# One query ring buffer, joined value products, two more blocks transposed by DMA, and a new order of work in a fused attention and gMLP kernel

## The chip, the cores and the metric

The kernel runs on one core of a Trainium2 chip. The metric is the device time of one execution in microseconds (us); for the kernel before it is the median of three runs.

## What is computed

`x` is 2048 tokens by 512 channels in bf16. After one layernorm without weights, two branches run on the same normalized input `xn`, and their outputs are added to `x`:

```python
def _A_ref(x, wqkv, wo):                 # 32 heads of 16, window of 256 tokens
    qkv = (x @ wqkv).reshape(B, S, 3, H, Dh) ...
    scores = einsum('bhqd,bhkd->bhqk', q, k) * Dh ** (-0.5)
    mask = (i - j >= 0) & (i - j < 256)
    p = softmax(where(mask, scores, -1e9))
    return einsum('bhqk,bhkd->bhqd', p, v) ... @ wo

def _B_ref(x, w_in, w_sp, b_sp, w_out):  # gMLP, 2 x 688 features
    z = gelu(x @ w_in); z1 = z[..., :688]; z2 = layernorm(z[..., 688:])
    g = einsum('ts,bsf->btf', w_sp, z2) + b_sp[None, :, None]
    return (z1 * g) @ w_out

xn = layernorm(x); return x + _A_ref(xn, ...) + _B_ref(xn, ...)
```

## The kernel before

The 2048 tokens are 16 blocks of 128 (`n`, also `qb` and `kb` for query and key blocks). The 32 heads are 4 groups `G` of 8; a group's projections are made for 512 tokens at a time (`grp`, 0 to 3).

**First stage (lines 211 to 373), in the order of the program.** SyncE (the queue SPq) loads `x` in pieces `xs` (two blocks each) and the two halves of `w_in` in two pieces each (`load_x`, L196; `load_win`, L204), then `wqkv`, the rest of `x`, and the output weights `wo_sb` and `w_out_sb` (L331 to L335). For each block, VectorE makes the statistics (`stats`, L254, L255, L119; the root is taken on GpSimd, L120) and the normalized block (`norm`, L260). Blocks 0 to 7 (`X_DMA = 8`) are transposed on TensorE (`transpose_x`, tile `tp`, L274) and copied out by ScalarE (L277); blocks 8 to 15 are transposed by a DMA that SPq issues (L265). Either way the result is `xnT`. `do_z(n, half)` multiplies a block with half of `w_in` in eight matmuls, four of 512 columns and four of 176 (tile `zs`, L285), and ScalarE applies the gelu (L293). TensorE works through this in program order: `z` of block `n`, half 1, comes two rounds after `norm(n)` has been issued. Twelve matmuls on zeros (`warm_up`, `N_WARM = (9, 3)`, L246) run ahead of and between the first two transposes. The first nine of 48 projections are done in this stage.

**Second stage: one list of tokens, `ORDER` (lines 49 to 65), played in order (lines 573 to 596).** Every engine gets its instructions in that order and keeps it. The tokens:

- `qIIe` is `scores(i, e)`: tile `i` of 45 holds four (key block, query block) pairs of the 180 that lie in the window, in the order of `BLOCKS`: per group, per key block, query blocks `kb`, `kb+1`, `kb+2`. For each of four heads, matmuls with 32 rows each (L483) fill half a tile `S` of the PSUM ring `ps_s`; two tiles are taken per call, and two exponentials on ScalarE (L491) of 128 x 1024 each turn them into `E`. Neighbouring pairs of one key block whose queries lie side by side in one tile `q` go into one matmul (`segs`); a query block with `qb % 4 == 0` starts a new one, as the next 512 queries are another tile.
- `mII` masks the tile: GpSimd for the diagonal blocks (L502), VectorE for `qb == kb + 2` (L507).
- `aGW`, `AGW`, `BGW`, `CGW` are `values`: for query blocks 2W and 2W+1 of group G, value products with 32 output rows each (L531), one per block pair, head and half: 1440 matmuls of 128 columns in all. `a` uses the one-bank pool `ps_y`, `A` and `C` a place of the ring `ps_s`. `divide` follows (L548 to L554), and `t` is `finish` (L565).
- `pKGg` and `PKGg` are the other projections (`proj`), in `ps_y` or in the ring.
- A number is that many `mix` steps (L402, 512 in all): the products with `w_sp`, 128 x 344 each. Sixteen of them end with an evacuation on VectorE (L409); at a row's end its `uT` is transposed by DMA (L425).
- `o` and `O` are halves of an output block (L433, L439), added to `x` on VectorE (L444) and stored (L445; blocks 13 to 15 from ScalarE's queue, the others from SPq).

`ps_s` has three places, `ps_y` and `ps_g` (for `mix`) one each. A score tile therefore waits until the exponential of the tile three places back in the ring has read it. Query tiles come from the pool `qp` of six, one per projection, in the order of the tokens.

Of the kernel before, what the change touches and what calls it, by code (L numbers as in the profile page):

```python
# [8 lines left out]
P = 128  # L9
BF = mybir.dt.bfloat16  # L10
# [5 lines left out]
D = 512  # L16
# [3 lines left out]
FH = 688  # L20
FQ = FH // 2
NB = S_TOK // P
# [6 lines left out]
Z_RANGES = [(0, 512), (512, FH)]  # L29
NRING = 6  # L30
EBUFS = 7
X_DMA = 8
LAST = 128
ONB = 4
N_WARM = (9, 3)

# [18 lines left out]
q171 t pq23 m15 2 t 2 q180 1 pq13 3 q181 6 m16 2 q190 a12 4 q191 1 m18 pq22 m19 3 q200 2 pv22 1  # L55
t 5 q201 a13 3 q210 2 m17 2 pq30 1 t q211 4 t 4 q220 pk23 C14 B15 q221 1 pk22 3 q230 7 m21 2
q231 3 pv23 q240 1 m22 m20 3 pv21 q241 5 Pk30 3 q250 t 4 a16 A17 q251 pv20 3 q260 8 m23 3 q261 2
pq31 q270 1 m25 m24 6 a20 q271 9 Pv31 q280 pv30 4 q281 1 m26 1 pk33 q290 9 Pq33 1 t q291 a21 t
A22 m27 4 q300 8 q301 4 pk32 q310 2 m28 5 t 2 q311 7 a23 q320 7 m29 7 q321 2 pk31 Pq32 1 m30 1
q330 6 t 4 q331 4 a24 q340 2 m33 m32 9 t q341 5 pv32 A25 q350 9 q351 5 m31 2 pv33 q360 t 8 q361  # L60
6 t 1 m34 1 a30 A26 t t q370 2 t t 1 a27 q371 5 m37 5 q380 2 o 1 q381 o m36 m35 10 q390 O O q391
t 6 a31 A32 q400 7 t 5 q401 3 o 1 q410 t o 4 m40 q411 o m39 3 q420 m38 o q421 5 O 4 O a33 q430
# [6 lines left out]
def kernel(  # L69
# [12 lines left out]
    nc = tc.nc  # L82
# [4 lines left out]
    pers = ctx.enter_context(tc.tile_pool(name="pers", bufs=1))  # L87
# [23 lines left out]
    qp = ctx.enter_context(tc.tile_pool(name="qp", bufs=NRING))  # L111
# [10 lines left out]
    q_t, k_t, v_t = {}, {}, {}  # L122

    def bank(name, ring):
        if ring:
# [3 lines left out]
    def proj(kind, G, grp, on_act=False, ring=False):  # L129
        m = bank("m", ring)  # L130
        if kind == "v":
            for j in range(4):
                n = 4 * grp + j
                for c in range(NDC):
                    nc.tensor.matmul(  # L135
                        m[:, j * P : (j + 1) * P], lhsT=xnT[:, c, n * P : (n + 1) * P],
                        rhs=wqkv[:, c, 2 * D + G * P : 2 * D + (G + 1) * P],
                        start=(c == 0), stop=(c == NDC - 1),
                    )
            t = v_bufs[(4 * G + grp) % NRING]  # L140
            v_t[(G, grp)] = t
            dst = t[:].rearrange("p n h a d -> p (n h) a d")[:, :, 0:3:2, :]
            src = m.rearrange("p (h e d) -> p h e d", e=2, d=DH)
            if on_act:
                nc.scalar.copy(out=dst, in_=src)
            else:
                nc.vector.tensor_copy(out=dst, in_=src)
            return
        w0 = (D if kind == "k" else 0) + G * P
        for c in range(NDC):  # L150
            nc.tensor.matmul(  # L151
                m, lhsT=wqkv[:, c, w0 : w0 + P], rhs=xnT[:, c, grp * 512 : (grp + 1) * 512],
                start=(c == 0), stop=(c == NDC - 1),
            )
        if kind == "q":
            t = qp.tile([P, 512], BF, name="q")
            q_t[(G, grp)] = t
            if on_act:
                nc.scalar.copy(out=t[:], in_=m)
            else:  # L160
                nc.vector.tensor_copy(out=t[:], in_=m)
# [15 lines left out]

    with tc.tile_pool(name="win_pool", bufs=1) as winp, tc.tile_pool(
# [152 lines left out]
        nc.sync.dma_start(out=wo_sb[:], in_=A_wo.rearrange("(c p) n -> p c n", p=P))  # L331
        nc.sync.dma_start(
            out=w_out_sb[:, 0:5, :], in_=B_w_out[0:640, :].rearrange("(c p) n -> p c n", p=P)
        )
        nc.sync.dma_start(out=w_out_sb[0 : FH - 5 * P, 5, :], in_=B_w_out[5 * P : FH, :])  # L335
        norm(2)
        do_z(1, 1)
        transpose_x(2)
# [123 lines left out]
    E_tiles = {}  # L462

    def scores(i, e):
# [4 lines left out]
        E = E_tiles[i]  # L469
        segs = []  # L470
        for j, (G, kb, qb) in enumerate(blocks):
            if segs and segs[-1][1:3] == [G, kb] and qb % 4:
                segs[-1][4] += 1
            else:
                segs.append([j, G, kb, qb, 1])
        tiles = []
        for pr in range(2):
            S = ps_s.tile([P, 2, 512], F32, name="S", tag="S")
            tiles.append(S)
            for h2 in range(2):  # L480
                s = 2 * pr + h2
                for j, G, kb, qb, w in segs:
                    nc.tensor.matmul(  # L483
                        S[:, h2, j * P : (j + w) * P],
                        lhsT=k_t[(G, kb // 4)][32 * s : 32 * s + 32, e, (kb % 4) * P : (kb % 4 + 1) * P],
                        rhs=q_t[(G, qb // 4)][32 * s : 32 * s + 32, (qb % 4) * P : (qb % 4 + w) * P],
                        start=True, stop=True,
                    )
        for pr in range(2):
# [26 lines left out]
    def values(G, w, home):  # L516
# [5 lines left out]
            tile2 = ps_s.tile([P, 2, 512], F32, name="o_t2", tag="S")  # L522
            Tb = tile2[:, 0, :]
        T = Tb.rearrange("p (e q) -> p e q", e=2)
        for j, qb in enumerate((2 * w, 2 * w + 1)):
            kbs = [kb for kb in (qb - 2, qb - 1, qb) if kb >= 0]
            for e in range(2):
                for kb in kbs:
                    i, b = INDEX[(G, kb, qb)]
                    for s in range(4):  # L530
                        nc.tensor.matmul(  # L531
                            T[32 * s : 32 * s + 32, e, j * P : (j + 1) * P],
                            lhsT=v_t[(G, kb // 4)][:, kb % 4, s, e : e + 2, :].rearrange("p a d -> p (a d)"),
                            rhs=E_tiles[i][:, 2 * s + e, b, :],
                            start=(kb == kbs[0]),
                            stop=(kb == qb),
                        )
        if home == "C":
            pair.append((G, w, tile2))
            return  # L540
# [26 lines left out]

    load_wsp(0)
    load_wsp(1)
    tokens = ORDER.split()  # L570
    last_proj = max(i for i, t in enumerate(tokens) if t[0] in "pP")
    xres = {}
# [54 lines left out]
```

## Time and profile before

| | |
|---|---|
| median of 3 runs | 267.56 us (267.45 to 267.75) |
| the profiled execution's own time | 268.1 us |
| its span, first to last instruction | 266.1 us |
| busy: TensorE, its weight loads, VectorE, ScalarE, GpSimd | 258.6, 147.1, 197.3, 206.0, 123.6 us |
| granted TensorE clock over the span | 1.00 |
| first exponential | 56.0 us into the span |

In the profile PE is TensorE's matmuls, PEld its weight loads, DVE VectorE, ACT ScalarE, POOL GpSimd, SPq SyncE's queue. A row of the timeline has the start, the length and the engine, line and tiles of some like instructions run together (`x8` is eight); the length reaches to the modelled end of the last one, which lies after the start of the next row, because matmuls are pipelined. The time that a piece of TensorE work takes is therefore read from start to start. A row of the chain of waits has the start, the length and the piece of work.

### The profile page before, as it was taken

The numbers are of one execution on the slowest core, as the hardware profiler recorded it, in microseconds if no ns is written. First come the engines' busy times: TensorE is split into PE (matmuls) and PEld (weight loads), VectorE is DVE, ScalarE is ACT, GpSimd is POOL, SyncE is SP. The second block draws the span as 40 slices with busy tenths as digits, with TensorE's granted clock in tenths as the row PEclk, the third lists the DMA queues.
The fourth block names the chain that finished last, engine by engine and source line by source line (L and its number), as shares of the span: only waits on it lengthen the run. The fifth ranks groups of instructions, "written<-read, shape, count | busy, mean of one in ns | idle before, by whom it ended". The sixth has DMA issues, their size and how long they took to land.

```text
span 266.1 us, 8418 instructions
## 1 busy us (share of the span) xinstructions
PE 258.6 (97%) x3661; PEld 147.1 (55%) x3694; DVE 197.3 (74%) x384; ACT 206.0 (77%) x235; POOL 123.6 (46%) x140
## 2 busy tenths in 40 slices
PE   7999999999999999999999999999999999999995
PEld 2565665645455547554656656655665454554543
DVE  5999999567766778968788888767777658568542
ACT  3677767699999999999999899897899789553000
POOL 4334454115645256746637493156573617247200
PEclk9999999999999999999999999999999999999999
DMA  6992325700504050251312054033059972423733
GB/s 204 350 363 55 61 40 112 88 2 2 110 15 98 2 111 21 63 46 38 81 31 52 17 66 81 2 81 83 15 130 272 143 123 59 98 74 30 150 91 89
DMA packets 60132, 23.63 MB, mean 89 GB/s; under 512 B 51216, under 2 KB 59584, under 8 KB 60096
## 3 DMA queue, kind: packets, MB, share of 16 engines
q1 hardware_dynamic: 59472, 22.70, 38.5%
q8 instruction: 29, 0.48, 0.7%
q10 hardware_dynamic: 576, 0.39, 0.5%
q0 software_dynamic: 48, 0.00, 0.3%
q14 instruction: 7, 0.06, 0.1%
HBM read 8.41 MB, written 2.10 MB: 39 GB/s over the span
## 4 chain that ended last, share of the span: by engine, by line
PE 88%; ACT 7%; DMA 2%; issue 1%; SPq 1%; DVE 0%; ACTq 0%
PE gf L402 28%; PE zs L285 14%; PE S L483 11%; PE m L151 8%; PE o_t L531 8%; PE fo L439 8%; ACT E L491 7%; PE m L135 5%; PE fo L433 5%; DMA w_in_sb<-in_B_w_in_dram 2%; PE tp L274 1%; ACT L491 0%; DVE xnT L444 0%; SPq L194 0%; SPq L196 0%
## 5 line engine op out<-in xcount | busy, mean ns | idle before, releaser
L491 ACT ACTIVATE E<-S 128x1024 bf16<-128x1024 f32 x180 | 168.4, 1056 | 18.1 <-PE S L483 14.1
L402 PE MATMUL gf<-z_all,wspT 128*128 128x344 bf16 x512 | 94.2, 310 | 0.0
L502 POOL TENSOR_SCALAR_AFFINE_SELECT E<-E 128x1024 bf16<-128x1024 bf16 x64 | 79.3, 1264 | 18.1 <-ACT E L491 18.0
L402 PEld LDWEIGHTS <-wspT 128*128 128x128 bf16 x512 | 44.2, 98 | 33.8 <-issue 10.5
L554 POOL TENSOR_TENSOR o_norm<-o_c,rsum 128x256 bf16<-128x256 f32 x32 | 23.2, 726 | 77.3 <-DVE rsum L552 77.3
L507 DVE TENSOR_TENSOR E<-E,fmask 128x1024 bf16<-128x1024 bf16 x56 | 51.9, 954 | 1.6 <-ACT E L491 1.5
L285 PE MATMUL zs<-w_in_sb,xnT 128*128 128x176 bf16 (+1 forms) x250 | 39.7, 307 | 0.7 <-DMA w_in_sb<-in_B_w_in_dram 0.4
L483 PE MATMUL S<-q,k 32*128 32x128 bf16 (+2 forms) x888 | 38.5, 251 | 0.8 <-ACT E L491 0.8
L293 ACT ACTIVATE z_all<-zs 128x688 bf16<-128x688 f32 x32 | 23.8, 744 | 12.5 <-PE zs L285 12.5
L151 PE MATMUL m<-xnT,wqkv 128*128 128x512 bf16 x110 | 31.3, 379 | 0.9
L285 PEld LDWEIGHTS <-xnT 128*128 128x128 bf16 x256 | 22.2, 98 | 15.3 <-issue 0.6
L409 DVE SCALAR_TENSOR_TENSOR z_all<-gf,b_all,z_all 128x344 bf16<-128x344 f32 x32 | 18.2, 570 | 15.8 <-PE gf L402 15.7
L483 PEld LDWEIGHTS <-k 32*128 32x128 bf16 x888 | 15.2, 92 | 25.7 <-issue 23.7
L548 DVE STREAM_TRANSPOSE o_c<-o_t 128x512 f32<-128x512 f32 x32 | 22.3, 698 | 8.2 <-PE o_t L531 8.0
L531 PE MATMUL o_t<-E,v 128*32 128x128 bf16 x1440 | 24.5, 220 | 0.0
L531 PEld LDWEIGHTS <-v 128*32 128x32 bf16 x1440 | 20.3, 97 | 6.2 <-issue 6.0
L439 PE MATMUL fo<-w_out_sb,uT 128*128 128x512 bf16 (+2 forms) x98 | 23.0, 366 | 0.3 <-issue 0.2
L444 DVE TENSOR_TENSOR xnT<-fo,xnT 128x512 bf16<-128x512 f32 (+2 forms) x17 | 11.1, 657 | 13.6 <-PE fo L439 13.6
L171 DVE TENSOR_TENSOR k<-m,emask 128x1024 bf16<-128x1024 f32 x13 | 15.8, 1219 | 6.3 <-PE m L151 6.3
L151 PEld LDWEIGHTS <-wqkv 128*128 128x128 bf16 x128 | 12.0, 98 | 11.3 <-issue 0.9
L120 POOL TENSOR_TENSOR rstdx<-rs_v,negh 128x1 f32<-128x1 f32 x16 | 10.3, 646 | 16.1 <-DVE rs_v L119 14.7
L298 DVE BATCH_NORM_STATS2 st<-z_all 128x6 f32<-128x344 bf16 x32 | 14.9, 506 | 3.7 <-ACT z_all L293 3.7
(51 smaller groups left out, 177.4 us busy)
## 6 DMA issues: line engine op xcount, KB each, us to landing
xnT<-in_A_x_dram SPq DMA_DIRECT2D x4, 512.0 KB, 6.4
xs<-in_A_x_dram SPq DMA_DIRECT2D x7, 256.0 KB, 7.5
out_dram<-xnT SPq DMA_DIRECT2D x13, 128.0 KB, 1.7
wqkv<-in_A_wqkv_dram SPq DMA_DIRECT2D x1, 1536.0 KB, 7.2
w_in_sb<-in_B_w_in_dram SPq DMA_DIRECT2D x4, 344.0 KB, 5.1
w_out_sb<-in_B_w_out_dram SPq DMA_DIRECT2D x1, 640.0 KB, 10.4
wo_sb<-in_A_wo_dram SPq DMA_DIRECT2D x1, 512.0 KB, 9.1
xs<-in_A_x_dram SPq DMA_DIRECT2D x2, 128.0 KB, 2.1
```

Source lines behind the costliest of these rows:

```text
L151: nc.tensor.matmul(m, lhsT=wqkv[:, c, w0 : w0 + P], rhs=xnT[:, c, grp * 512 : (grp + 1) * 512], start=(c == 0), stop=(c == NDC - 1),)
L285: nc.tensor.matmul(zp[:, lo:hi], lhsT=xnT[:, c, n * P : (n + 1) * P], rhs=w_in_sb[:, c, f0 + lo : f0 + hi], start=(c == 0), stop=(c == NDC ...
L293: nc.scalar.activation(out=dst[:, n, 0:FH], in_=zp[:, 0:FH], func=ACT.Gelu_apprx_tanh)
L402: nc.tensor.matmul(gf[:, 0:FQ], lhsT=wsp_tiles[n][:, c, :], rhs=z2_all[:, c, lo : lo + FQ], start=(c == 0), stop=(c == NB - 1),)
L439: nc.tensor.matmul(fo[:, c0:c1], lhsT=uT_tiles[n][:, c, :], rhs=w_out_sb[:, c, c0:c1], start=False, stop=(c == NFC - 1),)
L483: nc.tensor.matmul(S[:, h2, j * P : (j + w) * P], lhsT=k_t[(G, kb // 4)][32 * s : 32 * s + 32, e, (kb % 4) * P : (kb % 4 + 1) * P], rhs=q_ ...
L491: nc.scalar.activation(out=E[:, j : j + 3 : 2, 0:nb, :].rearrange("p h b c -> p h (b c)"), in_=tiles[pr][:, :, 0 : nb * P], func=ACT.Exp, ...
L502: nc.gpsimd.affine_select(out=E[:, :, j, :], in_=E[:, :, j, :], pattern=[[0, 8], [1, P]], compare_op=ALU.is_ge, fill=0.0, base=0, channel_ ...
L507: nc.vector.tensor_tensor(out=E[:, :, j, :], in0=E[:, :, j, :], in1=fmask[:].unsqueeze(1).to_broadcast([P, 8, P]), op=ALU.mult,)
L531: nc.tensor.matmul(T[32 * s : 32 * s + 32, e, j * P : (j + 1) * P], lhsT=v_t[(G, kb // 4)][:, kb % 4, s, e : e + 2, :].rearrange("p a d -> ...
L548: nc.vector.transpose(out=C[:, 0 : 32 * DH], in_=Tb)
L554: nc.gpsimd.tensor_tensor(out=o_n[:], in0=c_o.rearrange("p e q d -> p q e d"), in1=rsum[:].rearrange("p e q -> p q e").unsqueeze(3).to_bro ...
```

## The change

- **Queries.** The pool `qp` goes. All six tiles lie side by side in one buffer `q_ring`; group `G`, part `grp` has place `(4 * G + grp) % 6`. In `scores`, a matmul now goes on over the edge of 512 queries unless the ring wraps.
- **Value products.** `values` goes through half `e`, then key block, then query block, and joins the two query blocks of one key block into one matmul of 256 columns where they lie side by side in one tile `E`. Only the first step of a bank has `start`.
- **First stage.** `X_DMA` is 6: blocks 6 and 7 are transposed by DMA. The second piece of `w_in`'s half 1 is issued ahead of `load_x(1)`. One more warm-up matmul. `wo_sb` and `w_out_sb` are loaded after the first two `load_wsp`, just ahead of the token list.
- **End.** The first part of block 15 is stored from SPq instead of ScalarE's queue.
- **Order.** A new token list of the same work.

```diff
-X_DMA = 8
+X_DMA = 6
-N_WARM = (9, 3)
+N_WARM = (10, 3)
 ORDER = """
-pq10 Pk03 q000 1 pq03 2 q001 4 pk10 q010 9 m00 q011 pv11 m01 4 q020 4 pk11 q021 8 q030 a00 7
-q031 m02 1 pk12 2 q040 5 q041 1 m03 pq12 t 1 m04 3 q050 8 q051 pv03 4 q060 pq11 3 m05 q061 2 a01
-2 q070 9 q071 pv10 m06 4 q080 pk13 2 m07 1 q081 3 A02 2 q090 t a03 q091 4 A04 m08 q100 5 q101 3
-pk20 q110 5 t 3 t q111 pq20 4 q120 1 m10 pv13 4 q121 3 m11 a05 t q130 4 pv12 q131 8 t 1 q140 1
-m09 1 m12 1 pq21 q141 4 A06 a07 q150 8 q151 m13 a10 1 t 4 q160 3 pk21 2 q161 8 q170 m14 a11 6
...
-q330 6 t 4 q331 4 a24 q340 2 m33 m32 9 t q341 5 pv32 A25 q350 9 q351 5 m31 2 pv33 q360 t 8 q361
-6 t 1 m34 1 a30 A26 t t q370 2 t t 1 a27 q371 5 m37 5 q380 2 o 1 q381 o m36 m35 10 q390 O O q391
...
-m42 O 4 t 1 O 4 m41 1 o 2 q431 3 o 1 q440 C34 B35 t o q441 t m44 1 m43 1 o O 2 O 1 O 1 O 1 O 1
-A36 a37 2 O 1 t 1 o 1 o O t O 3 o o O O o o
+pv11 Pk03 q000 1 pq03 2 q001 2 pq10 1 q010 9 m00 q011 1 pk10 q020 3 m01 2 a00 1 q021 10 q030
+pk11 4 m02 q031 10 q040 2 pv03 q041 4 m03 t 1 pk12 q050 6 m04 1 q051 1 a01 3 q060 pk13 3 m05
+q061 4 a02 1 q070 8 q071 a03 1 t 3 q080 pv10 2 m07 2 q081 pq11 3 m06 1 q090 pq12 4 q091 a04 3
+m08 q100 2 pk20 2 q101 9 q110 pv12 1 t 1 m10 3 q111 1 pv13 1 m09 q120 5 pq21 q121 3 t 1 a05 m11
+q130 2 m12 8 q131 pq20 4 q140 t t 2 pk21 q141 3 A06 a07 A10 q150 4 m13 7 q151 2 pq13 q160 m14 6
...
+Pq33 3 a24 q321 2 t 7 t q330 3 pq32 t Pk31 q331 pv33 4 q340 2 m32 3 m33 3 q341 4 pv32 m34 1 q350
+2 t 10 q351 3 a30 A25 t A26 a27 q360 10 q361 3 t o 1 q370 1 m35 1 o m36 q371 3 m37 5 t q380 3 o
...
+q441 3 O m44 O o o t 5 A37 1 t O O t 2 o o 1 O O 6 O 1 O O O O O
 """
+    q_ring = pers.tile([P, NRING * 512], BF, name="q_ring")
         if kind == "q":
-            t = qp.tile([P, 512], BF, name="q")
+            at = (4 * G + grp) % NRING * 512
+            t = q_ring[:, at : at + 512]
         load_x(0, split=True)
         load_win(1, 0, 2)
+        load_win(1, 2, 4)
         load_x(1)
-        load_win(1, 2, 4)
-        nc.sync.dma_start(out=wo_sb[:], ...)          # these three go ...
-        nc.sync.dma_start(out=w_out_sb[:, 0:5, :], ...)
-        nc.sync.dma_start(out=w_out_sb[0 : FH - 5 * P, 5, :], ...)
-        (nc.scalar if n >= NB - 3 else nc.sync).dma_start(
+        (nc.scalar if n >= NB - 3 and c1 == D else nc.sync).dma_start(
         for j, (G, kb, qb) in enumerate(blocks):
-            if segs and segs[-1][1:3] == [G, kb] and qb % 4:
+            at = (4 * G + qb // 4) % NRING * 4 + qb % 4
+            if segs and segs[-1][1:3] == [G, kb] and at:
                 segs[-1][4] += 1
-                        rhs=q_t[(G, qb // 4)][32 * s : 32 * s + 32, (qb % 4) * P : (qb % 4 + w) * P],
+                        rhs=q_ring[32 * s : 32 * s + 32, at * P : (at + w) * P],
-        for j, qb in enumerate((2 * w, 2 * w + 1)):   # then e, kb, s: one matmul of 128 columns each
+        steps = []
+        for e in range(2):
+            for kb in range(max(0, 2 * w - 2), 2 * w + 2):
+                for qb in range(max(kb, 2 * w), min(kb + 3, 2 * w + 2)):
+                    i, b = INDEX[(G, kb, qb)]
+                    if qb > max(kb, 2 * w) and steps[-1][2:4] == [i, b - 1]:
+                        steps[-1][5] += 1
+                    else:
+                        steps.append([e, kb, i, b, qb - 2 * w, 1])
+        for n, (e, kb, i, b, j, l) in enumerate(steps):
+            for s in range(4):
+                nc.tensor.matmul(
+                    T[32 * s : 32 * s + 32, e, j * P : (j + l) * P],
+                    lhsT=v_t[(G, kb // 4)][:, kb % 4, s, e : e + 2, :].rearrange("p a d -> p (a d)"),
+                    rhs=E_tiles[i][:, 2 * s + e, b : b + l, :].rearrange("p b c -> p (b c)"),
+                    start=(n == 0), stop=(n == len(steps) - 1), skip_group_check=True,
+                )
     load_wsp(0)
     load_wsp(1)
+    nc.sync.dma_start(out=wo_sb[:], ...)              # ... and come here
+    nc.sync.dma_start(out=w_out_sb[:, 0:5, :], ...)
+    nc.sync.dma_start(out=w_out_sb[0 : FH - 5 * P, 5, :], ...)
```

More of the change, by code (lines that the diff above doesn't have):

```diff
@@ L56 @@
[L56 to L59, printed above, removed]
-q330 6 t 4 q331 4 a24 q340 2 m33 m32 9 t q341 5 pv32 A25 q350 9 q351 5 m31 2 pv33 q360 t 8 q361
-6 t 1 m34 1 a30 A26 t t q370 2 t t 1 a27 q371 5 m37 5 q380 2 o 1 q381 o m36 m35 10 q390 O O q391
@@ new lines @@
+m08 q100 2 pk20 2 q101 9 q110 pv12 1 t 1 m10 3 q111 1 pv13 1 m09 q120 5 pq21 q121 3 t 1 a05 m11
+q130 2 m12 8 q131 pq20 4 q140 t t 2 pk21 q141 3 A06 a07 A10 q150 4 m13 7 q151 2 pq13 q160 m14 6
+a11 q161 3 t 6 q170 1 t pv20 1 t q171 3 m16 5 m15 3 q180 4 pq23 q181 1 m17 8 q190 t a12 6 q191 1
+pk23 3 m18 3 q200 6 m19 4 q201 a13 C14 B15 q210 t 2 pv21 4 q211 5 m20 3 q220 2 pk22 Pv23 3 m21
+q221 3 pq31 q230 10 q231 pq30 2 m23 q240 4 pq22 2 m22 q241 7 t 1 q250 a16 1 t 3 q251 1 m24 2 t 3
+Pv30 6 q260 pk32 3 t q261 2 A20 a17 A21 q270 11 q271 m26 pk30 4 q280 t 10 q281 2 pv31 4 q290 1
@@ new lines @@
+m25 2 m28 7 q291 2 pv22 q300 1 m27 9 q301 m29 6 A22 m30 a23 q310 8 q311 3 t 5 pk33 q320 1 m31
+Pq33 3 a24 q321 2 t 7 t q330 3 pq32 t Pk31 q331 pv33 4 q340 2 m32 3 m33 3 q341 4 pv32 m34 1 q350
+2 t 10 q351 3 a30 A25 t A26 a27 q360 10 q361 3 t o 1 q370 1 m35 1 o m36 q371 3 m37 5 t q380 3 o
+1 q381 4 o q390 A31 a32 1 t 2 t 1 t q391 8 m39 q400 3 o 1 q401 o 1 O q410 2 O 1 o 3 m38 q411 1 o
+q420 1 m40 5 A33 a34 q421 O t 2 O 1 q430 2 t m42 m41 o 1 q431 2 o q440 m43 4 O 2 O 1 A35 a36
+q441 3 O m44 O o o t 5 A37 1 t O O t 2 o o 1 O O 6 O 1 O O O O O
@@ L120, in rpow @@
         nc.gpsimd.tensor_tensor(out=dst, in0=v[:, :n], in1=negh[:, :n], op=ALU.pow)
-    q_t, k_t, v_t = {}, {}, {}
+    k_t, v_t = {}, {}
     def bank(name, ring):
@@ L155, in proj @@
         if kind == "q":
-            t = qp.tile([P, 512], BF, name="q")
-            q_t[(G, grp)] = t
+            at = (4 * G + grp) % NRING * 512
+            t = q_ring[:, at : at + 512]
             if on_act:
-                nc.scalar.copy(out=t[:], in_=m)
+                nc.scalar.copy(out=t, in_=m)
             else:
-                nc.vector.tensor_copy(out=t[:], in_=m)
+                nc.vector.tensor_copy(out=t, in_=m)
             return
@@ L330 @@
             load_x(n2)
[L331 to L335, printed above, removed]
         norm(2)
@@ L481, in scores @@
                 s = 2 * pr + h2
-                for j, G, kb, qb, w in segs:
+                for j, G, kb, at, w in segs:
                     nc.tensor.matmul(
@@ L524, in values @@
         T = Tb.rearrange("p (e q) -> p e q", e=2)
-        for j, qb in enumerate((2 * w, 2 * w + 1)):
-            kbs = [kb for kb in (qb - 2, qb - 1, qb) if kb >= 0]
-            for e in range(2):
-                for kb in kbs:
+        steps = []
+        for e in range(2):
+            for kb in range(max(0, 2 * w - 2), 2 * w + 2):
+                for qb in range(max(kb, 2 * w), min(kb + 3, 2 * w + 2)):
                     i, b = INDEX[(G, kb, qb)]
[L530 to L537, printed above, removed]
+                    if qb > max(kb, 2 * w) and steps[-1][2:4] == [i, b - 1]:
[10 more added lines that the diff above has]
+                )
         if home == "C":
@@ L569 @@
     load_wsp(1)
+    nc.sync.dma_start(out=wo_sb[:], in_=A_wo.rearrange("(c p) n -> p c n", p=P))
+    nc.sync.dma_start(
+        out=w_out_sb[:, 0:5, :], in_=B_w_out[0:640, :].rearrange("(c p) n -> p c n", p=P)
+    )
+    nc.sync.dma_start(out=w_out_sb[0 : FH - 5 * P, 5, :], in_=B_w_out[5 * P : FH, :])
     tokens = ORDER.split()
```

5 lines of the change are left out of this document (1 added, 4 removed).

## The prediction

> **What bounds the kernel now.** I read the page first: busy time, then the chain of waits.
>
> ```profile
> span 266.1 us, 8418 instructions
> PE 258.6 (97%) x3661; PEld 147.1 (55%) x3694; DVE 197.3 (74%) x384; ACT 206.0 (77%) x235; POOL 123.6 (46%) x140
> PE 88%; ACT 7%; DMA 2%; issue 1%; SPq 1%; DVE 0%; ACTq 0%
> ```
>
> The chain that ends last is TensorE for 88% of the span and ScalarE for 7%. So the change is worth what it takes from TensorE's program, plus what it takes from the few places where TensorE stands still. Busy time cannot give the second, as a matmul's modelled end lies beyond the start of the next. I therefore read unit costs from start to start, in TensorE's timeline.
>
> ```profile
> 61.03 0.41 PE L483 MATMUL S<-q,k 32*128 32x256 bf16 x8
> 61.37 1.07 PE L135 MATMUL m<-wqkv,xnT 128*128 128x128 bf16 x16
> 62.28 0.75 PE L402 MATMUL gf<-z_all,wspT 128*128 128x344 bf16 x4
> 62.96 0.42 PE L483 MATMUL S<-q,k 32*128 32x128 bf16 x12
> 63.31 0.76 PE L402 MATMUL gf<-z_all,wspT 128*128 128x344 bf16 x4
> ...
> 65.21 1.34 PE L402 MATMUL gf<-z_all,wspT 128*128 128x344 bf16 x8
> 66.48 0.41 PE L483 MATMUL S<-q,k 32*128 32x384 bf16 x8
> 66.82 0.52 PE L531 MATMUL o_t<-E,v 128*32 128x128 bf16 x24
> 67.27 0.90 PE L402 MATMUL gf<-z_all,wspT 128*128 128x344 bf16 x5
> ```
>
> Four mix steps and the change to a score call take 62.96 - 62.28 = 0.68; eight take 66.48 - 65.21 = 1.27. So a mix step is 0.59 / 4, about 0.147, and what is left, 0.68 - 0.59, is 0.09: going from matmuls on the full array to 32-row score matmuls costs 0.09 to 0.10 by itself. I use 0.146 and 0.095. A score call of eight matmuls takes 61.37 - 61.03 = 0.34 with the change back, so 0.245 without; one of twelve takes 0.35. A v projection is 0.91.
>
> ```profile
> 72.53 0.86 PE m L151 x4
> 87.54 0.79 PE o_t L531 x48
> 109.75 1.45 PE o_t L531 x96
> ```
>
> From the chain: a q or k projection is 0.86. Value products: (1.45 - 0.79) / 48 = 0.0138 for one more matmul; 0.014 below.
>
> **Where TensorE stands still.** In the timeline some score calls take longer than 0.34. The first two of these rows are the two halves of one call; of the other two calls the first half and the work after the call are shown.
>
> ```profile
> 71.32 0.39 PE L483 MATMUL S<-q,k 32*128 32x256 bf16 x4
> ...
> 72.22 0.32 PE L402 MATMUL gf<-z_all,wspT 128*128 128x344 bf16 x1
> ...
> 88.66 0.39 PE L483 MATMUL S<-q,k 32*128 32x384 bf16 x4
> ...
> 89.63 0.85 PE L531 MATMUL o_t<-E,v 128*32 128x128 bf16 x48
> ...
> 92.23 0.40 PE L483 MATMUL S<-q,k 32*128 32x256 bf16 x4
> ...
> 93.30 0.76 PE L402 MATMUL gf<-z_all,wspT 128*128 128x344 bf16 x4
> ```
>
> These three calls (`q041`, `q090`, `q100`) take 0.90, 0.97 and 1.07, so TensorE loses 0.56 + 0.63 + 0.73 = 1.92. Their second half waits for an exponential to free a place of the ring; ScalarE meanwhile runs without a gap:
>
> ```profile
> 56.01 20.41 ACT L491 ACTIVATE E<-S 128x1024 bf16<-128x1024 f32 x22
> ```
>
> Less the last one's length (about 1.0) that is 19.4 / 21 = 0.923 from exponential to exponential, 1.846 for a score call. Early in the second stage the list gives TensorE less than 1.846 of work per call, so it runs ahead of ScalarE until the ring stops it.
>
> **The change part by part.** The sum is made on the profiled execution, 268.1 (span 266.1, 2.0 around it). That is 0.5 above the median of 267.56, and the difference that comes out is carried to the median.
>
> *Scores, -0.39.* Counted over `TILES`: of 90 calls, 54 have eight matmuls, 30 twelve and 6 sixteen; with the ring 82, 6 and 2. So 24 calls lose one step of four matmuls and 4 lose two (0.35 - 0.34 from the rows, 0.012 unrounded): 32 x 0.012 = 0.39. The columns stay the same.
>
> *Value products, -0.23.* 1440 matmuls of 128 become 720 of 128 and 360 of 256 columns, where the instruction count falls by 360 and the columns do not. What a matmul costs beside its columns shows in the two forms of the z product:
>
> ```profile
> L285 PE MATMUL zs<-w_in_sb,xnT 128*128 128x512 bf16 x122 | 37.6, 379 | 0.4 <-DMA w_in_sb<-in_B_w_in_dram 0.4
> L285 PE MATMUL zs<-w_in_sb,xnT 128*128 128x176 bf16 x128 | 30.6, 239 | 0.3
> ```
>
> (379 - 239) / (512 - 176) = 0.417 ns a column, so 128 columns are 53.3 ns. Value matmuls come four to 4 x 13.8 = 55 ns, on four strips of 32 outputs at once: streaming is nearly all of it, and 0.6 ns at most is left for each. 360 x 0.6 = 0.23. From below, nothing; the other bound is a rival.
>
> *Changes of the matmul's form, -0.38.* Going through both lists, leaving out `t` and `m`: 206 changes between full, score and value matmuls before, 202 after. 4 x 0.095.
>
> *Standing still, -1.4.* I add up TensorE's work from `q000` to each call and compare with 1.846 per call. The lead is largest at `q141`, the 30th call. Before: 10 q and k projections, 5 v, 140 mix steps, 29 calls, 264 value matmuls, 65 changes: 8.6 + 4.5 + 20.4 + 7.1 + 3.7 + 6.2 = 50.5, against 29 x 1.846 = 53.5, a lead of 3.0. After: 12, 4, 144, 29, the columns of 264, 67: 52.1, a lead of 1.4, and no call has more. Of 3.0 the three calls gave back 1.92, so some 1.1 goes free; then 0.3 is lost after. The ring's free lead shrinks by one exponential just behind an `A`, so I leave 0.5 and take 1.92 - 0.5 = 1.4. Bounds: 1.9 if all goes, 0 if it comes back elsewhere (a rival).
>
> *Start, +0.66, and transposes, -0.45.*
>
> ```profile
> 6.17 0.69 DVE L254 BATCH_NORM_STATS2 st<-xs 128x6 f32<-128x512 bf16 x1
> 6.55 0.75 PE L285 MATMUL zs<-w_in_sb,xnT 128*128 128x512 bf16 x4
> 7.72 1.91 PE L285 MATMUL zs<-w_in_sb,xnT 128*128 128x512 bf16 x12 [0.43 <-DMA w_in_sb<-in_B_w_in_dram]
> 8.19 0.41 DVE L260 TENSOR_SCALAR xn<-xs,mvx,rstdx 128x512 bf16<-128x512 bf16 x1
> 9.47 0.39 PE L274 MATMUL tp<-ident,xn 128*128 128x128 bf16 x4
> 9.69 1.39 PE L285 MATMUL zs<-w_in_sb,xnT 128*128 128x512 bf16 x8
> 10.94 0.38 PE L274 MATMUL tp<-ident,xn 128*128 128x128 bf16 x4
> ```
>
> ```profile
> 2.71 4.97 DMA w_in_sb<-in_B_w_in_dram
> ```
>
> Four z matmuls (0.58) from 6.55 end at 7.13, and the rest wait until 7.72 for the piece of `w_in` that lands at 2.71 + 4.97 = 7.68. Issued ahead of `load_x(1)` it lands before 7.13: -0.59. But `load_x(1)` then lands last, with the same bytes ahead of it, near 7.68, and VectorE's statistics of blocks 2 and 3 wait for it: they start at 7.71 instead of 6.17, `norm(2)` ends at 8.19 + 0.41 + 1.54 = 10.14, and its transpose starts at 10.2, while TensorE is there at 9.47 - 0.59 = 8.88. So it stands still for 1.33 at the new place: +0.74 net. The next z (10.94 - 9.69 = 1.25 for 1.17 of work) no longer waits for weights: -0.08. Bounds: -0.67 if `load_x(1)` is not later at all, +1.2 if it is later by half a us more. The tenth warm-up runs where TensorE waits for `norm(0)`: 0, at most one warm-up's 0.2. Blocks 6 and 7 take two groups of four transposes (9.69 - 9.47 = 0.22 each) off TensorE, and two copies off ScalarE, which waits for TensorE here.
>
> In their place come two DMAs:
>
> ```profile
> 16.15 0.41 DVE L260 TENSOR_SCALAR xn<-xs,mvx,rstdx 128x512 bf16<-128x512 bf16 x1
> 22.25 1.33 PE L285 MATMUL zs<-w_in_sb,xnT 128*128 128x512 bf16 x8
> ```
>
> ```profile
> xs<-in_A_x_dram SPq DMA_DIRECT2D x7, 256.0 KB, 7.5
> xnT<-xn SPq DMA_TRANSPOSE x8, 2.4
> ```
>
> `norm(6)` ends 1.54 later, at 18.1; 2.4 more is 20.5. Its z, at 22.25, comes at 22.25 + 0.66 - 0.45 = 22.5: two us hide the DMA. Behind it on SPq wait only later transposes. The Trainium skill (DMA: Bandwidth & Descriptors, Queues, rings and completion order) says that on each DMA engine descriptors are consumed in ring order. By that the transpose also stands behind the last `load_x`, which, issued near 11 and up to 1.5 later now, would land near 18.5 to 20, and the transpose as late as 22.4; the sum would be the same, without cover to spare. The output weights, moved, are used first near 200; `load_wsp` goes ahead of them. At the end, one store from SPq: 0.
>
> Sum: -0.39 - 0.23 - 0.38 - 1.4 + 0.66 - 0.45 = -2.2, so 265.9 profiled and **265.4** in the median; 263.9 to 266.8 with the bounds of start and standstill.
>
> **The rivals.**
>
> *The standstill moves* (0.15). The list is new everywhere, and VectorE and GpSimd free the banks. Nothing of the 1.4 comes: 266.8. For it, ScalarE's gapless row above; against, the smaller lead.
>
> *Masks come too late* (0.08, slower). Between a tile's last scores and the value products that need it lies less work now. `a30` needs tile 34: before, 9.9 of TensorE's work lay between (`q341` to `a30` in the list); after, 4 mix, a projection, a mix, two calls, 12 and 3 mix and changes: 4.9. `B15`, `A37`, `a00`, `a36` have 5.6 to 5.9; the least before was 8.5. Two exponentials (1.9) and two diagonal masks must fit:
>
> ```profile
> L502 POOL TENSOR_SCALAR_AFFINE_SELECT E<-E 128x1024 bf16<-128x1024 bf16 x64 | 79.3, 1264 | 18.1 <-ACT E L491 18.0
> L507 DVE TENSOR_TENSOR E<-E,fmask 128x1024 bf16<-128x1024 bf16 x56 | 51.9, 954 | 1.6 <-ACT E L491 1.5
> ```
>
> 1.9 + 2 x 1.26 = 4.4, under 4.9. It decides from queues of 0.5 on: with 2.0 of queue ahead the chain is 6.4, and these five lose 1.5 + 0.8 + 0.7 + 0.6 + 0.5 = 4.1: 269.5.
>
> *The ring buffer orders what it should not* (0.04, slower). If a score call waited for any newer write to `q_ring`, each of 13 query projections would hold the next call until VectorE's copy, about 0.9 less what lies between; the list has 0 to 4 mix steps there, some 8 in all: 273. Against it: pieces of `xnT` are written while others are read,
>
> ```profile
> 31.24 11.85 SPq L265 DMA_TRANSPOSE xnT<-xn  x5
> 31.79 1.41 PE L285 MATMUL zs<-w_in_sb,xnT 128*128 128x176 bf16 x9
> ```
>
> with no wait in the z products.
>
> *Value products go by the instruction* (0.03). If 14 ns were the price of each, joined or not, 360 fewer would give 5.0 instead of 0.23: 260.6. The Trainium skill (TensorE: Matmul & The Clock Gate, Part 1) has starts never closer than about 25 ns; by that the sum would be near 8 lower. The rows above have one per 14 ns, so the floor does not hold across strips, and the 55 ns for four fit the columns.
>
> **How the numbers follow.** Forecast 0.70, the rivals as given 0.30. 0.2% is 0.54 us, about what a measurement here can tell. The forecast's range lies below 267.0; of the moved standstill a quarter or more lies within 0.2%, as does the forecast's upper end. Faster 0.82, same 0.07, slower 0.11. The range takes in the moved standstill with a late start, and leaves out the other rivals: 263.8 to 267.2.
>
> **What would show it.** Right: no score call over 0.6 before 115; the first transpose after 9.0 waits for VectorE for about 1.3; 48 value matmuls' columns still take 0.78; z of block 6 without a wait; the first exponential near 56.2. Wrong: value products that start behind POOL or DVE masks, calls held by L161, or `load_x(1)` in time.

## The result, and the profile after

The changed kernel takes 266.47 us (median of 11 runs, 266.25 to 267.51); the kernel before, run beside it, 267.89 (11 runs, 267.45 to 268.86). The ratio is 0.9952, with a 95% interval of 0.9937 to 0.9967: faster, by 1.3 to 1.4 us. The forecast was 265.4 in a range of 263.8 to 267.2, and a gain of 2.2: the sign and the range held, and some two thirds of the gain came. The profiled execution is one of three of the eleven near 267.3; it took 267.51.

The page of the changed kernel, the rows that stand beside those of before:

```profile
span 265.8 us, 7432 instructions
PE 256.3 (96%) x3166; PEld 143.1 (54%) x3199; DVE 197.7 (74%) x384; ACT 205.6 (77%) x233; POOL 122.0 (46%) x140
q8 instruction: 25, 0.41, 0.7%
PE 93%; DMA 2%; DVE 1%; issue 1%; SPq 1%; DVEq 0%
```

ScalarE's 7% of the chain is gone. TensorE's timeline, around the two score calls before 115 that still take long, `q020` at 63.14 and `q080` at 85.37:

```profile
63.14 0.66 PE L479 MATMUL S<-q_ring,k 32*128 32x128 bf16 x8
63.74 0.90 PE L397 MATMUL gf<-z_all,wspT 128*128 128x344 bf16 x5
...
83.90 0.84 PE L532 MATMUL o_t<-E,v 128*32 128x128 bf16 x32
84.68 0.76 PE L397 MATMUL gf<-z_all,wspT 128*128 128x344 bf16 x4
85.37 0.44 PE L479 MATMUL S<-q_ring,k 32*128 32x128 bf16 x8
86.00 1.05 PE L135 MATMUL m<-wqkv,xnT 128*128 128x128 bf16 x16 [0.19 <-DVE o_c L548]
```

From start to start the two calls take 0.60 and 0.63, where 0.34 is the plain price. In `q020` the second half waits for the ring, which with 0.08 at another call (76.15) costs 0.34 in all, against 2.1 before (the three calls of the prediction and 0.16 at 111.13). In `q080` all eight score matmuls start within 0.12; what waits is the projection behind them, `pv10`, for VectorE's `o_c` to empty the one bank of `ps_y`, which `a03` had filled just before. That is 0.29 lost at a bank, and new with this list. And 48 value products' columns, now 32 matmuls, still take 84.68 - 83.90 = 0.78.

The start of the profiled execution, from the same timeline and from the chain of waits:

```profile
6.50 2.50 PE L285 MATMUL zs<-w_in_sb,xnT 128*128 128x512 bf16 x16
10.78 0.40 PE L274 MATMUL tp<-ident,xn 128*128 128x128 bf16 x4 [1.79 <-DVE xn L260]
```

```profile
2.71 5.55 DMA xs<-in_A_x_dram
```

The sixteen z matmuls run through, without the wait for `w_in`; then the transpose of block 2 waits 1.79 for VectorE, because `load_x(1)` landed at 2.71 + 5.55 = 8.26. That is later than the prediction's 7.68, and the first score matmul comes at 56.40, after 55.57 before. And near 200 there is a wait that nobody forecast:

```profile
201.63 0.41 PE L479 MATMUL S<-q_ring,k 32*128 32x384 bf16 x8
203.02 0.61 PE L397 MATMUL gf<-z_all,wspT 128*128 128x344 bf16 x3 [0.98 <-issue]
```

The mix step should start 0.34 after the score call, at 201.97, and starts at 203.02. "issue" says that nothing that the profile shows held it: no semaphore, no engine. (Such a mark can also be a missing record: the row at 163.69, a projection's, has 0.16 "issue" and three of its four matmuls. The rows read here have all of theirs.)

### The profile page after: what moved, and what is told of

It is laid out like the page before. It is cut to its first block, busy times and chain, and to the rows that moved or that the text cites. A ratio compares the mean times of both kernels' runs of the same rounds, so it can differ in the third digit from the quotient of the medians.

```text
span 265.8 us, 7432 instructions
## 1 busy us (share of the span) xinstructions
PE 256.3 (96%) x3166; PEld 143.1 (54%) x3199; DVE 197.7 (74%) x384; ACT 205.6 (77%) x233; POOL 122.0 (46%) x140
## 4 chain that ended last, share of the span: by engine, by line
PE 93%; DMA 2%; DVE 1%; issue 1%; SPq 1%; DVEq 0%
PE gf L397 31%; PE zs L285 13%; PE S L479 12%; PE m L151 10%; PE o_t L532 8%; PE fo L434 8%; PE m L135 6%; PE fo L428 5%; DMA xs<-in_A_x_dram 2%; DVE st L254 0%; PE tp L274 0%; SPq L204 0%; DVE xnT L439 0%; SPq L194 0%; DVE o_c L548 0%
## 5 line engine op out<-in xcount | busy, mean ns | idle before, releaser
L503 DVE TENSOR_TENSOR E<-E,fmask 128x1024 bf16<-128x1024 bf16 x56 | 52.6, 967 | 2.6 <-ACT E L487 2.5
L554 POOL TENSOR_TENSOR o_norm<-o_c,rsum 128x256 bf16<-128x256 f32 x32 | 21.5, 671 | 62.0 <-DVE rsum L552 59.3
L285 PE MATMUL zs<-w_in_sb,xnT 128*128 128x512 bf16 (+1 forms) x249 | 39.1, 307 | 0.4
L479 PE MATMUL S<-q_ring,k 32*128 32x128 bf16 (+2 forms) x760 | 37.2, 267 | 0.0
L479 PEld LDWEIGHTS <-k 32*128 32x128 bf16 x760 | 12.7, 92 | 25.9 <-issue 25.2
L532 PE MATMUL o_t<-E,v 128*32 128x128 bf16 (+1 forms) x1080 | 23.4, 238 | 0.0
L532 PEld LDWEIGHTS <-v 128*32 128x32 bf16 x1080 | 19.2, 97 | 5.1 <-issue 4.6
L135 PE MATMUL m<-wqkv,xnT 128*128 128x128 bf16 x256 | 16.9, 219 | 0.2 <-DVE o_c L548 0.2
```

Source lines behind the costliest of these rows:

```text
L135: nc.tensor.matmul(m[:, j * P : (j + 1) * P], lhsT=xnT[:, c, n * P : (n + 1) * P], rhs=wqkv[:, c, 2 * D + G * P : 2 * D + (G + 1) * P], st ...
L285: nc.tensor.matmul(zp[:, lo:hi], lhsT=xnT[:, c, n * P : (n + 1) * P], rhs=w_in_sb[:, c, f0 + lo : f0 + hi], start=(c == 0), stop=(c == NDC ...
L479: nc.tensor.matmul(S[:, h2, j * P : (j + w) * P], lhsT=k_t[(G, kb // 4)][32 * s : 32 * s + 32, e, (kb % 4) * P : (kb % 4 + 1) * P], rhs=q_ ...
L503: nc.vector.tensor_tensor(out=E[:, :, j, :], in0=E[:, :, j, :], in1=fmask[:].unsqueeze(1).to_broadcast([P, 8, P]), op=ALU.mult,)
L532: nc.tensor.matmul(T[32 * s : 32 * s + 32, e, j * P : (j + l) * P], lhsT=v_t[(G, kb // 4)][:, kb % 4, s, e : e + 2, :].rearrange("p a d -> ...
```

## The experiments

Times are medians; each ratio is to the kernel before run on the same chip (267.93 to 268.2).

**1. Is the profiled execution typical?** The changed kernel again, unaltered.

> The changed kernel once more, unaltered, as the reference for the runs beside it. One theory: the 1.05 us in which TensorE stood before a mix step at 201.83 in the first profile, with no wait on that instruction, is an accident of some executions (of 11 times, 8 lie at 266.3 to 266.8 and 3 at 267.2 to 267.5); then it may be missing in this profile, and the span is then near 264.7. The rival: it belongs to the order and stands at the same place again, and the span is near 265.8. Both: the second transpose group's wait for VectorE's norm(2) is there again, 1.9 us, and the first score matmul starts near 56.4.

Measured: 266.22 (8 runs), ratio 0.9944 (0.9923 to 0.9965). TensorE's timeline and the chain of waits of this execution, whose span is 264.5:

```profile
195.87 2.50 PE L532 MATMUL o_t<-E,v 128*32 128x128 bf16 x120
198.30 0.41 PE L479 MATMUL S<-q_ring,k 32*128 32x384 bf16 x8
198.64 1.63 PE L397 MATMUL gf<-z_all,wspT 128*128 128x344 bf16 x10
200.21 0.41 PE L479 MATMUL S<-q_ring,k 32*128 32x384 bf16 x8
201.77 0.61 PE L397 MATMUL gf<-z_all,wspT 128*128 128x344 bf16 x3 [1.16 <-issue]
```

```profile
2.71 4.13 DMA xs<-in_A_x_dram
```

The late start belongs to that execution: here `load_x(1)` lands at 6.84, the transpose of block 2 waits 0.29, and the first score matmul starts at 54.97. (Of the 19 times of these two series five are above 267; of those, one alone has a profile.) The wait near 200 belongs to the kernel: 201.77 - 200.21 - 0.34 = 1.22.

**2. The start's order of loads.** The old order back in the changed kernel.

```diff
         load_win(1, 0, 2)
-        load_win(1, 2, 4)
         load_x(1)
+        load_win(1, 2, 4)
```

> The changed kernel with the old order of the first loads: load_x(1) ahead of the second piece of w_in. The theory that the start is where the expected gain went: the wait of 1.95 before the transpose of block 2 goes and the wait of 0.59 for w_in comes back, so the first score matmul comes 1.2 to 1.3 earlier than in the changed kernel (near 55.15), and the time falls by 1.0 to 1.3 to about 265.2. The rival, that the start is hidden and ScalarE's exponentials or the ring set the pace behind it: less than 0.4.

Measured: 266.27 (6 runs), ratio 0.9931 (0.9911 to 0.9951); first score matmul at 54.95. The expectation fell: this edit of the change is worth nothing that shows, either way. With the old order the z matmuls wait 0.34 for `w_in`, with the new one the transpose 0.29 for VectorE.

**3. The transposes of blocks 6 and 7 back on TensorE.**

```diff
-X_DMA = 6
+X_DMA = 8
```

> The changed kernel with blocks 6 and 7 transposed on TensorE again. By the two groups of four transposes at 0.22 each: slower by 0.45. If VectorE, and not TensorE, sets the pace of the first stage: the same within 0.2.

Measured: 267.40 (11 runs), ratio 0.9976 (0.9967 to 0.9985). The first score matmul starts at 55.72, 0.75 later than in run 1; from there to the last matmul both take 206.2 to 206.3. But 0.30 of the 0.75 is there before blocks 6 and 7 have any work. TensorE's timeline at the fourth group of transposes (block 3) and at the first score call, in run 1:

```profile
10.76 0.39 PE L274 MATMUL tp<-ident,xn 128*128 128x128 bf16 x4
...
54.97 0.41 PE L479 MATMUL S<-q_ring,k 32*128 32x384 bf16 x8
```

and with `X_DMA = 8`:

```profile
11.06 0.38 PE L274 MATMUL tp<-ident,xn 128*128 128x128 bf16 x4
...
55.72 0.41 PE L479 MATMUL S<-q_ring,k 32*128 32x384 bf16 x8
```

From the one row to the other it is 54.97 - 10.76 = 44.21 and 55.72 - 11.06 = 44.66, so the two DMAs are worth 0.45, as forecast. All fourteen profiles agree: 44.6 to 44.7 in the four with eight blocks transposed on TensorE, 44.2 in the ten with six. The ratios say 0.9 (0.9976 less 0.9944), with intervals that reach 0.45.

**4. The value products alone, and the order alone.** Single value products in the changed kernel (`a_no_join`), the old list in it (`a_old_order`), and the new list in the kernel before (`b_new_order`).

```diff
-        steps = []
-        ...
+        for j, qb in enumerate((2 * w, 2 * w + 1)):
+            ...                  # e, kb, s as before: one matmul of 128 columns each
```

> The changed kernel with the value products as they were: 1440 matmuls of 128 columns, query block by query block, each block pair by itself. If streaming sets their rate: slower by 0.2 to 0.3 us. The rival that a value matmul has a price by itself: slower by up to 5.0.

> The changed kernel with the old token list. If the counted work and the standstill are right: four more changes of the matmul's form (0.38) and the three long score calls near 71, 88 and 92 come back (1.4 to 1.9 in all), so slower than the changed kernel by 1.8 to 2.3, about 268.3. If the standstill only moved with the new list: slower by 0.4 alone.

> The kernel before with the new token list alone. If the new list needs the joined products because runs of 120 to 168 value products empty TensorE's instruction supply: slower than the kernel before, by 4 to 5, about 272.5. If the list's smaller standstill is what counts: faster, by 1.4 to 1.8.

Measured: `a_no_join` 272.38 (5 runs), ratio 1.0172 (1.0147 to 1.0196); `a_old_order` 266.79 (8), 0.9959 (0.9943 to 0.9975); `b_new_order` 272.66 (4), 1.0169 (1.0149 to 1.0189). So under the new list joining is worth 6 us where 0.23 was forecast; without joining the new list costs 4.5; and with it the list is worth only 0.4 (by the ratios, whose intervals overlap) to 0.7 (206.91 less 206.22 from the first score matmul to the last matmul) where 1.8 was forecast. TensorE's timeline in `b_new_order`:

```profile
198.98 0.41 PE L483 MATMUL S<-q,k 32*128 32x128 bf16 x11
203.55 0.23 PE L483 MATMUL S<-q,k 32*128 32x128 bf16 x1 [4.17 <-issue]
203.71 3.05 PE L402 MATMUL gf<-z_all,wspT 128*128 128x344 bf16 x10
206.69 0.59 PE L483 MATMUL S<-q,k 32*128 32x128 bf16 x10
```

and in `a_no_join`:

```profile
197.51 2.24 PE L527 MATMUL o_t<-E,v 128*32 128x128 bf16 x146
203.26 0.51 PE L527 MATMUL o_t<-E,v 128*32 128x128 bf16 x22 [3.51 <-issue]
```

The same kind of wait, at the same place, but of 4.4 and 3.7 us, before the last matmul of a score call and in the middle of a run of value products. Neither stands where work goes on to a new bank. In `a_old_order` it is missing, and the ring is full again:

```profile
87.85 0.39 PE L479 MATMUL S<-q_ring,k 32*128 32x384 bf16 x4
88.51 0.40 PE L479 MATMUL S<-q_ring,k 32*128 32x384 bf16 x4 [0.27 <-ACT E L487]
...
91.42 0.39 PE L479 MATMUL S<-q_ring,k 32*128 32x256 bf16 x4
92.18 0.40 PE L479 MATMUL S<-q_ring,k 32*128 32x256 bf16 x4 [0.37 <-ACT E L487]
```

**What the wait is.** The busy table over the stretch that ends inside the wait counts what TensorE has begun by then (length, then PE and PEld with their numbers, and the other engines): the changed kernel, the one with `X_DMA = 8`, and `b_new_order`.

```profile
0.00:202.50 202.50, 197.18 (x2503) 113.01 (x2527) 162.66 (x326) 173.62 (x200) 99.65 (x119) 1.00 0.41 90
```

```profile
0.00:201.50 201.50, 198.21 (x2503) 113.90 (x2527) 162.37 (x326) 174.14 (x201) 99.28 (x119) 1.00 0.38 89
```

```profile
0.00:201.00 201.00, 196.35 (x2887) 115.40 (x2911) 162.05 (x325) 173.31 (x200) 99.27 (x118) 1.00 0.38 89
```

`X_DMA = 8` has eight more transposes at the start, and its wait comes eight score matmuls earlier in the list (between the ten mix steps and the score call): the same 2503 matmuls and 2527 loads. `b_new_order` has 384 matmuls and 384 loads more, which is 3 x 256 instructions; `a_no_join`, counted in the same way, 256 and 256 more, 2 x 256. `a_no_join` has two shorter waits of the kind, of 0.65 and 0.91:

```profile
137.65 0.40 PE L479 MATMUL S<-q_ring,k 32*128 32x384 bf16 x4 [0.27 <-issue]
...
161.86 1.34 PE L397 MATMUL gf<-z_all,wspT 128*128 128x344 bf16 x8 [0.74 <-issue]
```

They come 8 x 128 and 5 x 128 weight loads ahead of its long one. (Loads are counted here as none of their records is missing.) So the wait stands at a fixed edge of TensorE's own program, every 256 instructions, whatever work lies there. The queue that the page calls q8 "instruction" moved 25 packets of 16 KB after and 29 before:

```profile
q8 instruction: 29, 0.48, 0.7%
```

That is (3166 + 3199) / 25 = 255 and (3661 + 3694) / 29 = 254 of TensorE's instructions for each. The transfers of the changed kernel in the stretch from 197.5 to 200.5 and in the one from 200.5 to 203 (packets, MB, share of 16 engines):

```profile
q1 hardware_dynamic: 1073, 1.07, 108.9%
```

```profile
q1 hardware_dynamic: 913, 0.53, 145.5%
q8 instruction: 1, 0.02, 2.8%
```

From 197.5 to 200.5 the data of the 2 MB reload of `x` (`xnT`, four pieces issued together) keep the DMA engines full, and no block of q8 comes; the next one comes after 200.5. Read from the records of the transfers (us), with the matmuls counted in steps of 128 from the one that waited:

```
                    edge before   next block's   TensorE reaches   goes on   wait
                    is passed     DMA starts     the next edge     at
changed kernel         197.5        200.6           202.0           203.0     1.05
again                  196.1        199.3           200.6           201.8     1.2
X_DMA = 8              196.8        199.7           201.0           202.2     1.2
a_no_join              197.8        200.9           199.5           203.3     3.7
b_new_order            197.2        201.1           199.2           203.6     4.4
```

In each of them TensorE goes on 2.4 to 2.6 us after that DMA started (2.9 and 3.4 at the two shorter waits of `a_no_join`). So the wait is (start of the block's DMA + 2.5) less the time at which TensorE reaches the edge. Two things make it: the block's DMA starts 2.9 to 3.9 after the edge before is passed, beside the reload, where none of the other 24 blocks of the changed kernel's profile starts more than 2.2 after its edge; and a run of value products uses the instructions up, 120 matmuls and their loads in 198.30 - 195.87 = 2.43, where 128 mix steps with their loads would take 128 x 0.147 = 19. `a_old_order` has the first without the second: its reload is issued at 195.8, and the block due at the edge of 201.6 starts at 205.6, 4.0 late, but its TensorE reaches the next edge only at 213.1 and doesn't wait. The Trainium skill (Runtime: NRT & Kernel Launch, Instruction fetch mechanics) says that each engine refills its instruction memory in blocks of 256 by a DMA queue of its own, while it runs, and calls the cost of an edge mostly hidden; the blocks of 256 agree with these traces, the hidden cost holds in all but these places, where it is 0.65 to 4.4 us. The same section gives TensorE's memory 2048 instructions; a reserve of that size isn't seen here, since TensorE stops 256 instructions after the edge at which the late block fell due.

**5. Take the reload away from there.** The first piece of the reload stays; the other three are issued some tokens later each.

```diff
-            for c in range(NDC):
-                nc.sync.dma_start(out=xnT[:, c, :]..., in_=x2...[c])
+            x_due = {i: 0, tokens.index("q361") + 1: 1, tokens.index("q370") + 1: 2, tokens.index("q380") + 1: 3}
+        if i > last_proj and i in x_due:
+            c = x_due[i]
+            nc.sync.dma_start(out=xnT[:, c, :]..., in_=x2...[c])
```

> The changed kernel with its reload of x (four DMAs of 512 KB into xnT, issued together behind the last projection) spread: the first piece where it was, the others behind q361, q370 and q380. Theory: TensorE stands for 1.05 to 1.22 before a mix step near 200 because its next instructions, which a DMA of 16 KB brings, are held up behind the 2 MB (that DMA starts 495 TensorE instructions after the one before, against about 256 elsewhere). Then the long score call near 200 is back to 0.34 and the time falls by 1.0 to 1.2, to about 265.1. Rival: what TensorE misses there is a place of the ring or an evacuation on VectorE; then the stall stays and the time with it.

> The changed kernel with single value products and with the spread reload of x. In the kernel with single value products alone TensorE stood for 3.7 inside a run of 168 value products near 200. If its instructions came late behind the reload: most of 3.7, and the slower clock behind it (1.3), goes, about 268.0 to 268.5. If so many short instructions in a row are too many for the refill in any case: at least 2 of the 3.7 stay, above 270.

> The kernel before with its reload of x spread, the first piece where it was, the others behind q371, q380 and q390. In the profile of before an instruction DMA of TensorE also came late beside the reload (419 instructions after the one before it), but TensorE did not stand. If the spread is worth something only where TensorE runs out of instructions: the same within 0.3. If the 2 MB at once cost something else too (late wspT, late stores): faster by 0.5 or more.

Measured: on the changed kernel 265.37 (4 runs), ratio 0.9898 (0.9883 to 0.9913), 0.9 less than in run 1 (1.2 by the ratios); on `a_no_join` 267.65 (10), 0.9981 (0.9965 to 0.9997), 4.7 less; on the kernel before 268.06 (12), 1.0007 (0.9997 to 1.0016), nothing. TensorE's timeline in the first:

```profile
200.47 0.41 PE L479 MATMUL S<-q_ring,k 32*128 32x384 bf16 x8
200.81 0.61 PE L397 MATMUL gf<-z_all,wspT 128*128 128x344 bf16 x3
```

The wait is gone (200.81 - 200.47 = 0.34): the block's DMA now starts at 196.5, 0.2 after its edge. With single products it starts 0.8 after, and the wait falls from 3.7 to 1.2:

```profile
200.38 0.51 PE L527 MATMUL o_t<-E,v 128*32 128x128 bf16 x22 [0.96 <-issue]
```

So the second theory of that run was right in part. Single value products use up 256 instructions in 128 x 0.0138 = 1.8 us, and a block brings new ones 2.2 us or more after its DMA has started, so TensorE would wait even for a block that starts at its edge; the two shorter waits stay too, with about 0.7 and 0.3. With the reload spread joining is still worth 2.3 (267.65 less 265.37). In the kernel before the reload holds a block back as well (its DMA starts at 207.8, 5.4 after the edge at 202.3), but TensorE reaches the next edge at 213.3, so there is nothing to gain. That the reload holds the block back is shown by this; how it does so (a place in a queue, a share of the engines) is not.

**6. The score matmuls, and the place of the edges.** Broken at each 512 queries again, first alone, then with the spread reload.

```diff
-            if segs and segs[-1][1:3] == [G, kb] and at:
+            if segs and segs[-1][1:3] == [G, kb] and qb % 4 and at:
```

> The changed kernel with the ring buffer for the queries, but with score matmuls broken at each 512 queries again (888 for 760). By the counted steps: slower by 0.39. If the shorter program matters through TensorE's instruction supply near 200: more, up to 1. If the ring buffer is the cost and the joins are nothing: the same.

> The changed kernel with both edits that took the stall near 200 away: score matmuls broken at each 512 queries again, and the reload of x spread over the list. Theory: breaking the score matmuls gained 0.95 only because it moved the place at which TensorE's instructions are fetched again; with the reload spread there is no stall to lose, so breaking now costs what the prediction gave for it, 0.39: 265.37 + 0.39 = 265.8 (ratio to the kernel before 0.9910 to 0.9925), TensorE's program from first score to last matmul 205.4, no stall near 200. Rival 1: broken matmuls are no dearer than joined ones, the saving of 0.39 was never there: 265.4. Rival 2: broken score matmuls are faster by themselves, and the two gains add: 264.3. Rival 3: where refills fall decides more than either, and a stall shows at another place: over 266.2.

Measured: alone 265.27 (4 runs), ratio 0.9906 (0.9893 to 0.9918): faster than the changed kernel by about 1, which nothing had foreseen. There is no wait near 200:

```profile
200.42 0.42 PE L479 MATMUL S<-q_ring,k 32*128 32x128 bf16 x12
200.77 0.61 PE L397 MATMUL gf<-z_all,wspT 128*128 128x344 bf16 x3
```

More instructions ahead of it move the edges: counted in weight loads they lie at 197.0 and 204.7 now, and the late block (its DMA starts at 200.4, as late as ever) is there in time. With the spread reload as well: 265.73 (5 runs), ratio 0.9914 (0.9900 to 0.9927). The two gains don't add, and breaking now seems to cost what was forecast (the ratios' intervals overlap): from the first score matmul to the last matmul TensorE takes 205.34 instead of 205.03, 0.31 for the 0.39 forecast.

**7. Joining under the old list.** `a_old_order` with single value products.

> The changed kernel with the old token list and single value products. If the joining is worth its 0.2 to 0.3 where no run of value products is long (at most 96 in the old list): slower than the changed kernel with the old list alone by 0.2 to 0.3, about 267.0. If a value product has a price by itself: by 5 to 6, as with the new list.

Measured: 267.27 (10 runs), ratio 0.9978 (0.9962 to 0.9995), against 266.79 and 0.9959; the stretch from first score to last matmul 207.06 against 206.91. So 0.15 in the traces and 0.5 in the medians, whose intervals overlap: where instructions come in time, joining is worth about what its streaming gives.

## Why the prediction was right, and where it was off

Read from the timelines (us), the profile of before against that of run 1 and of the spread reload:

```
                                    before    again    spread reload
first score matmul starts            55.57    54.97    55.20
last matmul starts                  262.87   261.20   260.23
between                             207.30   206.23   205.03
```

**The second stage, forecast -0.39 - 0.23 - 0.38 - 1.4 = -2.40.** Without the late block it is 205.03 - 207.30 = -2.27: the four terms together were right. The ring gave back 2.1 - 0.34 = 1.7, and the wait of `pv10` for a bank took 0.29 of it again: 1.45 (forecast 1.4). Joined scores are worth 0.31 (0.39). The old list in the changed kernel takes 206.91, so the new one is worth 206.91 - 205.03 = 1.88 where nothing waits for instructions, and 1.4 + 0.38 = 1.78 was forecast for it. Single value products cost 0.15 under the old list (0.23).

**What failed is the step that a standing time which goes stays gone.** With the late block the stage is -1.07: 1.2 of the 2.4 came back at 200. A rival had this (the standstill moves, 266.8, 0.15), and its time was near, but it named VectorE and GpSimd and their banks; they end the 0.29 at `pv10`, and no row of theirs ends the wait at 200. The trace of before shows the transfers of q8, 29 packets, one of them 5.4 after its edge beside the same reload, and the edges could have been laid over the new list's run `a30 A25 t A26 a27` of value products; the prediction counted value products by their columns alone. For the same reason "value products, -0.23" was right as streaming and wrong as the worth of the edit in this list: single products there cost 6 us, of which 3.7 - 1.2 is the longer wait at 200, 0.65 and 0.91 are the two shorter ones, and 1.5 is the clock (below).

**The start, +0.66, was mis-sized; the transposes, -0.45, were not.** Together they give 54.97 - 55.57 = -0.60, where +0.21 was forecast. The transposes are 0.4 of it, read from the fourth group of transposes to the first score matmul (44.21 in run 1, 44.63 before). What is left for the start is 10.76 - 10.94 = -0.18; in the profiles of the changed kernel's variants that group starts at 10.6 to 11.1, and only in the first profile later, at 12.18. The step that failed: `load_x(1)`, issued last, was to land where the second piece of `w_in` had landed, at 7.68, as the bytes ahead of it are the same. In run 1 it landed at 6.84 and in the profiled execution at 8.26; the landing of one piece in one profile was no figure to carry over. Experiment 2 shows no worth in the order itself. So 0.8 too much at the start and 1.2 too little at 200 cancelled in great part: that the total came near is luck, and the forecast looks better than its parts.

**What would show it.** Calls over 0.6 before 115: one, `q080` with 0.63, and its wait is a projection's for a bank. First transpose after 9.0 waiting for VectorE about 1.3: 1.79 in one profile and 0.29 in the other. 48 value columns at 0.78: yes. z of block 6 without a wait: yes. First exponential near 56.2: 56.84 with the late start, 55.41 in run 1. Rivals: no value product waited for a mask, no score call for `q_ring`, and value products don't go by the instruction, as 32 joined and single matmuls take the 0.78 of 48. Two sums of the prediction are off: 360 starts of 25 ns are 9.0, so that price would lower the sum by 8.8 and not near 8, and the bounds of start and standstill, added plainly, give 263.5 to 267.3 and not 263.9 to 266.8. Neither changes the forecast.

**Versions that beat both kernels**: the changed kernel with the reload spread (265.37) or with the score matmuls broken (265.27). The second is luck of where the edges fall; the first takes the cause away.

## What to carry to other kernels

Small matmuls that run side by side used up instructions faster than any other work here: where hundreds of them follow each other, join them where their operands allow it, look at what the DMA engines carry just then, and keep large transfers that aren't urgent out of that stretch or in pieces. A wait that ends with "issue" with no matmul's record missing, that stands at the same instruction count in variants of a kernel and moves by whole multiples of 256 between others, points to the instruction supply; the starts of the blocks' DMAs, and a run that moves the transfer away, settle it. And an edit that changes the number of instructions ahead of such a place moves it, so a gain of a microsecond from an edit that should cost one is a reason to look for this.

## What was not expected of the hardware

TensorE's instructions came by DMA while the kernel ran, and a transfer of data held them up: beside 2 MB the DMA of a block of 256 started 2.9 to 3.9 us after its edge, instead of 0.2 with the transfer spread, and the wait that followed was 1.05 to 4.4 us. Such a wait can cost twice. After the wait of 4.4 us in `b_new_order` ten mix steps take 206.69 - 203.71 = 2.98 instead of 1.46, and the busy table shows the granted clock (the last column but two):

```profile
203.70:205.40 1.70, 1.70 (x7) 0.89 (x7) 0.19 (x1) 1.02 (x1) 0.00 (x0) 0.51 1.08 236
205.40:207.40 2.00, 2.00 (x19) 0.84 (x18) 0.00 (x0) 0.06 (x1) 0.00 (x0) 0.56 0.00 0
207.40:209.00 1.60, 1.55 (x15) 0.70 (x14) 0.00 (x0) 1.60 (x2) 0.00 (x0) 1.00 0.00 0
```

It is half until about 207 and whole again after. The same followed the wait of 3.7 us in `a_no_join`, and none of those of 1.2 us. The Trainium skill (TensorE: Matmul & The Clock Gate, What's actually happening) gives one idle window of about 3.4 us as what halves the clock; the five waits of the table agree with it.
